# Transposing q and k by crossbar DMA instead of on TensorE, and reading q in row order in the score matmul

## The chip, the cores and the metric

The kernel runs on one core of a Trainium2 chip. The metric is the device time of one execution in microseconds (us), the median of three runs. TensorE (PE) does the matmuls, VectorE (DVE), ScalarE (ACT) and GpSimd (POOL) the elementwise work; SP and GpSimd issue the DMAs.

## The reference, cut to what matters

A sliding-window attention with a linear distance bias, and behind it a two-layer network with ELU, on all tokens:

```python
B, H, S, D = 8, 8, 576, 64                       # q, k, v: float32
scores = q @ k.T / sqrt(D)                       # per batch and head
bias = slope[h] * -abs(i - j)
mask = (0 <= i - j) & (i - j < 128)              # window of 128 keys
attn = softmax(where(mask, scores + bias, -1e9))
x = attn @ v                                     # (B*S, H*D) = (4608, 512)
h = x @ w_in                                     # 512 -> 2048
g = where(h > 0, h, exp(min(h, 0)) - 1)
out = g @ w_out                                  # 2048 -> 512, (4608, 512) float32
```

## The kernel before, in words

**Slots.** The order of the work is written out by hand. The dictionary `tasks` and the function `at(s, f, ...)` (L510) put calls into numbered slots, and the loop at L589 issues slot after slot. A batch takes 16 slots, batch b the slots 16b to 16b+15. In each slot stand, in this order on TensorE: one hidden group (`hidden`, x by w_in into a bank of PSUM, L451), the value matmuls of the slot before (`values`, L394), the score matmuls of this slot (`scores`, L348), transposes if there are any, and one output group of four matmuls (`output`, g by w_out, L492). Each engine takes its instructions in the order in which they are issued.

**Scores.** Keys stand on the partitions of the result and queries on its columns. The 576 rows are cut into blocks of 128 and a last one of 64; a slot has four score matmuls of 128 columns (slots 0 to 13 of a batch), or eight of 64 columns (slots 14 and 15). So there are 56 matmuls of 128 columns in a batch. ScalarE takes the exponential (L372), VectorE cuts off what lies outside the window by a minimum with `band` (`cut`, L380). In batch 0 the bias is added by further matmuls (L368); from batch 1 on it stands in rows 64 to 127 of QK as extra terms of the product.

**The order of rows.** q and k are loaded by GpSimd (`load_qk`, L80) so that partition p gets rows 4p to 4p+3: a run of 1 KB per head, converted to float16. Transposing 128 columns of this (two rows of 64) on TensorE gives columns for rows 4p+j. `transposes` (L307) does it for two heads at a time, eight matmuls (L312) into a PSUM tile of the ring that the scores use too (two buffers, tag "sps"). Two copies per call bring it into QK, by ScalarE for odd pairs of heads (L322) and by VectorE for even ones (L324). In QK the rows of a block of 128 stand in the order j, i: all rows 4i, then all 4i+1, and so on. So the attention's result, x, and the output have their rows in this order too. v is placed in it as well (`place_v4`, L116, batches 0 to 2; `load_v` and `cast_v`, L126 and L134, from batch 3 on). A store of 128 rows of `out` is therefore cut into pieces by `rows_of` (L467): four of 32 rows with a step of four rows in HBM, or fewer where the last block of 64 rows is in it (L498).

**Where the preparation stands.** For batch b+1 the four calls of `transposes` stand in slots 5, 9, 10 and 13 of batch b (9, 10, 13 and 14 of batch 1; 14, 14, 15, 15 of batch 0), and `transposes_tail` for the last 64 rows in slot 14.

**Behind the attention.** `normalize` (L414, L415) divides by the row sums into xn; one slot later `turn` (L418) brings xn into the ring xT, which the hidden groups read: by TensorE in batches 0 and 1, by a crossbar transpose on SP's queue (L423) from batch 2 on. ScalarE takes exp of the hidden group (L455), GpSimd cuts it to 0 to 1 (L456), VectorE makes g (`elu`, L463) one slot later. The hidden groups have two buffers in PSUM.

**Queues.** SP issues the loads of v from batch 3 on, the turns of xn and the stores. GpSimd issues the loads of q and k, the tails and v of the first batches, between its own work: e (L456) and casts of v (L134).

Of the kernel before, what the change touches and what calls it, by code (L numbers as in the profile page):

```python
# [9 lines left out]
F16 = mybir.dt.float16  # L10
I32 = mybir.dt.int32
AF = mybir.ActivationFunctionType
ALU = mybir.AluOpType
# [6 lines left out]
def kernel(  # L20
# [9 lines left out]
    nc = tc.nc  # L30
    B, H, S, D = q.shape
    NTOK, DO = out.shape
    FF = moe_w_in.shape[1]
    NP = H // 2
# [6 lines left out]
    V = nc.vector  # L41

    const = ctx.enter_context(tc.tile_pool(name="const", bufs=1))
    stage = ctx.enter_context(tc.tile_pool(name="stage", bufs=2))
# [8 lines left out]
    def one(shape, dt, name):  # L53
        return const.tile(shape, dt, name=name, tag=name)
# [18 lines left out]

    stq, stt, vf, vs = {}, {}, {}, {}

# [73 lines left out]
    with tc.manual_schedule():  # L149

        row = one([128, 1], I32, "row")
        col = one([128, 128], I32, "col")
        posi = one([128, 576], I32, "posi")
        nc.gpsimd.iota(row, pattern=[[0, 1]], base=0, channel_multiplier=1)
        nc.gpsimd.iota(col, pattern=[[1, 128]], base=0, channel_multiplier=0)
        load_half(0, 1, 0)
# [16 lines left out]
        rowf = small("rowf")  # L173
        V.tensor_copy(rowf, row)
        V.tensor_scalar(out=ident, in0=col, scalar1=rowf, scalar2=None, op0=ALU.is_equal)
        for h in range(H):
# [25 lines left out]

        seen(0, posi[:, 0:256], kpos, 0, 256)
        unseen(0, 128, 0.0, ALU.is_gt)
# [3 lines left out]
        def last_blocks():  # L208
            seen(256, posi[:, 512:576], kpos, -384, 64)
            seen(320, posi[:, 512:576], rowf, -512, 64)  # L210
            unseen(256, 64, -127.0, ALU.is_lt)
            unseen(320, 64, 0.0, ALU.is_gt)
            join(256, 128)
# [93 lines left out]
        def transposes(b, hp):  # L307
# [8 lines left out]
            for odd in range(2):  # L316
# [6 lines left out]
                else:  # L323
                    V.tensor_copy(o, i)  # L324

        def transposes_tail(b):
            t = ps_s.tile([128, NP, 2, 64], F16, name="tpt", tag="sps")
# [12 lines left out]
        def scores(b, s):  # L340
# [6 lines left out]
            def mm(o, h, kc, qc, n):  # L347
                nc.tensor.matmul(t[:, o:o + n], qk[0:r, h, 1, kc:kc + 128], qk[0:r, h, 0, qc:qc + n],  # L348
                                 start=b > 0 or o == 0, stop=b > 0)
# [116 lines left out]

        def rows_of(c0):  # L467

            r = []
            c = c0  # L470
            while c < c0 + 128:
                b, o = divmod(c, S)
                if o < 512:
                    n, p = divmod(o, 128)
                    r.append((c - c0, out[b * S + 128 * n + p // 32:b * S + 128 * n + 128:4, :]))
                    c += 32
                else:
                    r.append((c - c0, out[c:c + 64, :]))
                    c += 64
            return r  # L480

        def output(t, j):
# [11 lines left out]
            if f0 == 12:  # L494
                ob = work.tile([128, DO], F32, name="ob", tag="ob")
                nc.scalar.copy(ob, ops[t])  # L496
                for p0, rows in rows_of(512 * t + 128 * ts):
                    nc.sync.dma_start(rows, ob[p0:p0 + rows.shape[0], :])  # L498

# [10 lines left out]
        def at(s, f, *a):  # L510
            tasks.setdefault(s, []).append((f, a))
# [15 lines left out]
        for b in range(B):  # L527
# [16 lines left out]
            if b + 1 < B:  # L544
                for hp in range(NP):
                    at(s0 + ((5, 9, 10, 13) if b > 1 else (9, 10, 13, 14) if b else (14, 14, 15, 15))[hp],
                       transposes, b + 1, hp)
                at(s0 + (14 if b else 25), transposes_tail, b + 1)
# [34 lines left out]
        at(18, load_v4, 2)  # L583
        at(33, load_v4_tail, 2)
        for n in range(4):
            at(15 + n, place_v4, 1, n)
            at(32 + n, place_v4, 2, n)

# [39 lines left out]
```

The softmax here doesn't subtract the row's maximum and nothing guards it: scores larger than these inputs give would overflow.

## Time and profile before

| | |
|---|---|
| median of the runs | 366.17 us (366.01 to 367.24) |
| the profiled execution | 365.46 us, its span 363.7 us |
| TensorE busy | 340.3 us |
| VectorE busy | 243.5 us |
| ScalarE busy | 206.7 us |
| GpSimd busy | 145.7 us |
| transposes L312, in number | 224 (7 batches of 32) |
| stores, in number | 136 |

A line of a group gives: line, engine, operation, output <- input, shapes, count, then busy us and mean ns of one, then the engine's idle time just before them and what ended it. A line of a timeline gives start, us, engine, line, operation, and in brackets idle time before it and its releaser. Matmuls are pipelined: the mean time of one contains its latency, and the pace of a stream is read from the starts. A digit of the slices is the busy share of a fortieth of the span, in tenths.

### The profile page before, as it was taken

The numbers are of one execution on the slowest core, as the hardware profiler recorded it, in microseconds if no ns is written. First come the engines' busy times: TensorE is split into PE (matmuls) and PEld (weight loads), VectorE is DVE, ScalarE is ACT, GpSimd is POOL, SyncE is SP. The second block draws the span as 40 slices with busy tenths as digits, with TensorE's granted clock in tenths as the row PEclk, the third lists the DMA queues.
The fourth block names the chain that finished last, engine by engine and source line by source line (L and its number), as shares of the span: only waits on it lengthen the run. The fifth ranks groups of instructions, "written<-read, shape, count | busy, mean of one in ns | idle before, by whom it ended". The sixth has DMA issues, their size and how long they took to land.

```text
span 363.7 us, 9613 instructions
## 1 busy us (share of the span) xinstructions
PE 340.3 (94%) x3790; PEld 251.6 (69%) x3790; DVE 243.5 (67%) x574; ACT 206.7 (57%) x349; POOL 145.7 (40%) x229
## 2 busy tenths in 40 slices
PE   6878997999979999989999999999999999999994
PEld 6766775777647667767777777777777777666651
DVE  6479889678886776666676767776776756634430
ACT  4355583666537655765566665666567565543431
POOL 9146623434314723472346334642433232233320
PEclk9899999999999999999999999999999999999999
DMA  8999999839243973497448934793631222211113
GB/s 114 198 206 119 228 107 183 151 80 155 38 103 89 133 108 84 110 128 110 98 94 127 127 88 100 120 136 82 102 84 45 52 47 45 51 43 47 29 43 73
DMA packets 81948, 37.06 MB, mean 102 GB/s; under 512 B 51952, under 2 KB 77296, under 8 KB 81904
## 3 DMA queue, kind: packets, MB, share of 16 engines
q0 software_dynamic: 34064, 15.40, 35.5%
q1 hardware_dynamic: 47840, 21.06, 25.6%
q8 instruction: 29, 0.48, 0.6%
q14 instruction: 15, 0.12, 0.1%
HBM read 36.70 MB, written 9.44 MB: 127 GB/s over the span
## 4 chain that ended last, share of the span: by engine, by line
PE 65%; DVE 14%; ACT 9%; DMA 7%; issue 3%; POOL 1%; SPq 0%; ACTq 0%; POOLq 0%
PE hp L451 27%; PE op L492 25%; PE sp L348 5%; ACT QK L322 5%; DVE VP L116 4%; DMA vs<-in_v_dram 3%; PE av L394 3%; DVE g L463 3%; ACT EX L372 2%; DVE QK L324 2%; ACT e L455 2%; DVE EX L380 2%; DMA xT<-xn 2%; DMA stq<-in_q_dram 1%; DVE xn L415 1%
## 5 line engine op out<-in xcount | busy, mean ns | idle before, releaser
L456 POOL TENSOR_SCALAR e<-e 128x512 f32<-128x512 f32 x144 | 88.6, 615 | 199.9 <-ACT e L455 199.9
L451 PE MATMUL hp<-xT,wi 128*128 128x256 f16 (+3 forms) x1536 | 150.3, 246 | 8.1 <-DVE g L463 3.6
L451 PEld LDWEIGHTS <-wi 128*128 128x128 f16 x1536 | 121.5, 98 | 49.9 <-DVE g L463 5.5
L455 ACT ACTIVATE e<-hp 128x512 f32<-128x512 f32 x144 | 86.0, 597 | 119.0 <-PE hp L451 110.0
L492 PE MATMUL op<-wo,g 128*128 128x512 f16 x576 | 146.4, 379 | 0.0
L463 DVE SCALAR_TENSOR_TENSOR g<-e,hp 128x512 f16<-128x512 f32 x144 | 98.0, 681 | 23.9 <-POOL e L456 22.7
L380 DVE TENSOR_TENSOR EX<-EX,band 128x512 f16<-128x512 f16 x112 | 49.8, 445 | 57.1 <-ACT EX L372 57.0
L372 ACT ACTIVATE EX<-sp 128x512 f16<-128x512 f32 x128 | 75.9, 593 | 13.3 <-PE sp L368 8.6
L492 PEld LDWEIGHTS <-g 128*128 128x128 f16 x576 | 51.2, 98 | 36.9
L348 PE MATMUL sp<-QK 128*128 128x128 f16 (+3 forms) x576 | 49.8, 213 | 0.0
L394 PE MATMUL av<-VP,EX 128*128 128x65 f16 x576 | 38.6, 193 | 4.3 <-DVE EX L380 2.7
L394 PEld LDWEIGHTS <-EX 128*128 128x128 f16 x576 | 31.6, 98 | 8.7 <-DVE EX L380 4.2
L415 DVE TENSOR_TENSOR xn<-av,rden 128x256 f16<-128x256 f32 x80 | 34.0, 424 | 2.8
L348 PEld LDWEIGHTS <-QK 128*128 128x128 f16 (+1 forms) x576 | 31.3, 97 | 1.0 <-issue 0.2
L496 ACT COPY ob<-op 128x512 f32<-128x512 f32 x36 | 21.1, 586 | 14.3 <-PE op L492 6.4
L322 ACT COPY QK<-tp 64x1024 f16<-64x1024 f16 x28 | 28.1, 1005 | 1.6 <-PE tp L312 1.4
L414 DVE RECIPROCAL rden<-av 128x4 f32<-128x4 f32 x80 | 14.4, 180 | 16.0 <-PE av L394 14.6
L134 POOL TENSOR_SCALAR VP<-vf 128x512 f16<-128x512 f32 (+1 forms) x25 | 19.5, 779 | 2.7 <-DMA vf<-in_v_dram 2.7
L324 DVE COPY QK<-tp 64x1024 f16<-64x1024 f16 x28 | 19.2, 684 | 1.1 <-PE tp L312 0.8
L312 PE MATMUL tp<-ident,stq 128*128 128x128 f16 x224 | 17.1, 219 | 2.3 <-ACT QK L322 1.0
L312 PEld LDWEIGHTS <-stq 128*128 128x128 f16 x224 | 13.8, 98 | 3.4 <-issue 3.2
L116 DVE COPY VP<-vs 32x512 f16<-32x512 f16 x48 | 14.9, 310 | 1.3 <-DMA vs<-in_v_dram 0.5
(70 smaller groups left out, 118.5 us busy)
## 6 DMA issues: line engine op xcount, KB each, us to landing
out_dram<-ob SPq DMA_DIRECT2D x128, 64.0 KB, 1.7
vf<-in_v_dram SPq DMA_DIRECT2D x80, 64.0 KB, 2.3
stq<-in_k_dram POOLq DMA_DIRECT2D x7, 512.0 KB, 6.4
stq<-in_q_dram POOLq DMA_DIRECT2D x7, 512.0 KB, 7.5
wi<-in_moe_w_in_dram POOLq DMA_DIRECT2D x4, 512.0 KB, 13.8
wo<-in_moe_w_out_dram POOLq DMA_DIRECT2D x4, 512.0 KB, 15.1
QK<-TQ SPq DMA_DIRECT2D x2, 576.0 KB, 8.0
vs<-in_v_dram POOLq DMA_DIRECT2D x2, 512.0 KB, 9.9
```

The source lines that it names most:

```text
L312: nc.tensor.transpose(t[:, g, w, :, j, :], stq[b][:, w, 2 * hp + g, 2 * j:2 * j + 2, :].rearrange("p a d -> p (a d)"), ident)
L322: nc.scalar.copy(o, i)
L348: nc.tensor.matmul(t[:, o:o + n], qk[0:r, h, 1, kc:kc + 128], qk[0:r, h, 0, qc:qc + n], start=b > 0 or o == 0, stop=b > 0)
L372: nc.scalar.activation(e[:, 0:512], t, AF.Exp, scale=0.125)
L380: V.tensor_tensor(out=e, in0=e, in1=band[:, c:c + n].unsqueeze(1).broadcast_to([128, 512 // n, n]), op=ALU.min)
L394: nc.tensor.matmul(a[:, l, :], e[:, c:c + 128], vp[:, n, h, 0:D + 1], start=st, stop=sp)
L415: V.tensor_tensor(out=xnt[b, i][:, 4 * half:4 * half + 4, :], in0=a[:, :, 0:D], in1=r.unsqueeze(2).broadcast_to([128, 4, D]), op=ALU.mult)
L451: nc.tensor.matmul(p[:, l * w + u0:l * w + u1], w_in_sb[:, c, fc * 128:(fc + 1) * 128], xT[:, c, x0:x0 + u1 - u0], start=(c == 0), stop=(c ...
L455: nc.scalar.activation(e, p, AF.Exp)
L456: nc.gpsimd.tensor_scalar(out=e, in0=e, scalar1=1.0, scalar2=0.0, op0=ALU.min, op1=ALU.max)
L463: V.scalar_tensor_tensor(out=gs[t][:, f0:f0 + nf, c0:c0 + w], in0=sh(es.pop((t, j))), scalar=1.0, in1=sh(hps.pop((t, j))), op0=ALU.subtrac ...
L492: nc.tensor.matmul(ops[t], gs[t][:, fc, ts * 128:(ts + 1) * 128], w_out_sb[:, fc, :], start=(fc == 0), stop=(fc == NFC - 1))
```

## The change

For batches 2 to 7 `transposes` is no longer called. In its place stand two new functions, eight calls of each per batch:

- `cross(b, n)` issues one crossbar transpose on SP's queue: from 128 partitions of stq, two heads of q or of k (512 columns of float16), to the tile tq in SBUF, of which there is one buffer. For batches 3 to 7 they stand in slots 0 to 7 of the batch before, for batch 2 in slots 22 to 25, two in each.
- `uncross(b, n)` copies from tq to QK on VectorE, for one j and all heads: 64 partitions by 1024 elements, float16, SBUF to SBUF. They stand in slots 5 to 12 of the batch before, for batch 2 in slots 28 to 31, two in each.

The layout of QK stays as it was. The score matmuls with 128 columns now read q through a rearranged pattern: four elements with a step of 32, then the next four. So the columns of the scores, and all that follows from them, have q's rows in their own order; the window and the distances of the first blocks are made from `col` instead of `posi`. Each store of 128 rows is one DMA, and `rows_of` is gone. The tail load of v of batch 2 moves from slot 33 to 22, and its placement from slots 32 to 35 to slots 24, 26, 28 and 30.

```diff
-        col = one([128, 128], I32, "col")
+        col = one([128, 256], I32, "col")
...
-        seen(0, posi[:, 0:256], kpos, 0, 256)
+        seen(0, col, kpos, 0, 256)
...
+        def cross(b, n):
+
+            w, hp = 1 - n // NP, n % NP
+            if n == 0:
+                tq[b] = stage.tile([128, 2, H, 2, 128], F16, name="tq", tag="tq", bufs=1)
+            nc.sync.dma_start_transpose(
+                out=tq[b][:, w, 2 * hp:2 * hp + 2, :, :].rearrange("p h a c -> p (h a) c"),
+                in_=stq[b][:, w, 2 * hp:2 * hp + 2, :, :].rearrange("p h j d -> p (h j d)"))
+
+        def uncross(b, n):
+            w, j = 1 - n // 4, n % 4
+            r = slice(64 * (j % 2), 64 * (j % 2) + 64)
+            V.tensor_copy(
+                QK[b % 2][0:64, :, w, 0:512].rearrange("p h (n j i) -> p h n j i", j=4, i=32)[:, :, :, j, :],
+                tq[b][r, w, :, j // 2, :].rearrange("p h (n i) -> p h n i", i=32))
...
-                nc.tensor.matmul(t[:, o:o + n], qk[0:r, h, 1, kc:kc + 128], qk[0:r, h, 0, qc:qc + n],
+                m = qk[0:r, h, 0, qc:qc + n]
+                if n == 128:
+                    m = m.rearrange("p (j i) -> p i j", j=4)
+                nc.tensor.matmul(t[:, o:o + n], qk[0:r, h, 1, kc:kc + 128], m,
                                  start=b > 0 or o == 0, stop=b > 0)
...
-                for p0, rows in rows_of(512 * t + 128 * ts):
-                    nc.sync.dma_start(rows, ob[p0:p0 + rows.shape[0], :])
+                r = 512 * t + 128 * ts
+                nc.sync.dma_start(out[r:r + 128, :], ob)
...
-                for hp in range(NP):
-                    at(s0 + ((5, 9, 10, 13) if b > 1 else (9, 10, 13, 14) if b else (14, 14, 15, 15))[hp],
-                       transposes, b + 1, hp)
+                if b == 0:
+                    for hp in range(NP):
+                        at((14, 14, 15, 15)[hp], transposes, b + 1, hp)
+                else:
+                    for n in range(8):
+                        at(s0 + (n if b > 1 else 6 + n // 2), cross, b + 1, n)
+                        at(s0 + (5 + n if b > 1 else 12 + n // 2), uncross, b + 1, n)
...
-        at(33, load_v4_tail, 2)
+        at(22, load_v4_tail, 2)
         for n in range(4):
             at(15 + n, place_v4, 1, n)
-            at(32 + n, place_v4, 2, n)
+            at(24 + 2 * n, place_v4, 2, n)
```

More of the change, by code (lines that the diff above doesn't have):

```diff
@@ L71 @@
     xT = one([128, 4, RING], F16, "xT")
-    stq, stt, vf, vs = {}, {}, {}, {}
+    stq, stt, vf, vs, tq = {}, {}, {}, {}, {}
     def load_qk(b, w, h0=0, h1=H):
@@ L151 @@
         row = one([128, 1], I32, "row")
-        col = one([128, 128], I32, "col")
+        col = one([128, 256], I32, "col")
         posi = one([128, 576], I32, "posi")
         nc.gpsimd.iota(row, pattern=[[0, 1]], base=0, channel_multiplier=1)
-        nc.gpsimd.iota(col, pattern=[[1, 128]], base=0, channel_multiplier=0)
+        nc.gpsimd.iota(col, pattern=[[1, 256]], base=0, channel_multiplier=0)
         load_half(0, 1, 0)
@@ L174 @@
         V.tensor_copy(rowf, row)
-        V.tensor_scalar(out=ident, in0=col, scalar1=rowf, scalar2=None, op0=ALU.is_equal)
+        V.tensor_scalar(out=ident, in0=col[:, 0:128], scalar1=rowf, scalar2=None, op0=ALU.is_equal)
         for h in range(H):
@@ L208, in last_blocks @@
         def last_blocks():
-            seen(256, posi[:, 512:576], kpos, -384, 64)
-            seen(320, posi[:, 512:576], rowf, -512, 64)
+            seen(256, col[:, 0:64], kpos, 128, 64)
+            seen(320, col[:, 0:64], rowf, 0, 64)
             unseen(256, 64, -127.0, ALU.is_lt)
@@ L465, in elu @@
                 in1=sh(hps.pop((t, j))), op0=ALU.subtract, op1=ALU.max)
[L467 to L480, printed above, removed]
         def output(t, j):
```

## The prediction

> **What bounds the kernel now.** I read the page first: busy shares, slices, chain, groups.
>
> ```profile
> PE 340.3 (94%) x3790; PEld 251.6 (69%) x3790; DVE 243.5 (67%) x574; ACT 206.7 (57%) x349; POOL 145.7 (40%) x229
> PE   6878997999979999989999999999999999999994
> DMA  8999999839243973497448934793631222211113
> PE 65%; DVE 14%; ACT 9%; DMA 7%; issue 3%; POOL 1%; SPq 0%; ACTq 0%; POOLq 0%
> ```
>
> TensorE is full from about slice 8 on. A busy TensorE need not be TensorE at its peak, so I looked in the timeline for the pace of one slot: from one hidden group to the next.
>
> ```profile
> 244.35 1.04 PE L451 MATMUL hp<-xT,wi 128*128 128x256 f16 x8
> 245.22 0.29 PE L394 MATMUL av<-VP,EX 128*128 128x65 f16 x4
> 245.35 0.38 PE L348 MATMUL sp<-QK 128*128 128x128 f16 x4
> 245.57 1.03 PE L492 MATMUL op<-wo,g 128*128 128x512 f16 x4
> 246.44 1.04 PE L451 MATMUL hp<-xT,wi 128*128 128x256 f16 x8
> ```
>
> The starts are 2.09 us apart with no wait in brackets. The four score matmuls hold the engine from 245.35 to 245.57: 0.22 us, 55 ns each. A slot with transposes looks so:
>
> ```profile
> 228.34 0.39 PE L348 MATMUL sp<-QK 128*128 128x128 f16 x4
> 228.93 0.61 PE L312 MATMUL tp<-ident,stq 128*128 128x128 f16 x8 [0.21 <-ACT QK L322]
> 229.38 1.03 PE L492 MATMUL op<-wo,g 128*128 128x512 f16 x4
> ```
>
> Eight transposes hold TensorE for 0.45 us, and before them it waits 0.21 us for a score buffer that ScalarE still empties. The kernel has its own control: while batch 7 is scored, nothing is left to transpose. In the same timeline, hidden groups 16 slots apart start at 242.15 and 278.94 (batch 6 scored, batch 7 prepared: 36.79 us), then at 278.94 and 312.63 (batch 7 scored: 33.69 us). Preparing a batch so costs 3.10 us: 4 x 0.45 = 1.80 of transposes, 0.33 of tail transposes (which stay), the rest, 0.97, waits around the copies.
>
> The groups by line and the DMA issues of the page price what is exchanged (count, busy us, mean ns; for a DMA the us from issue to landing), and the waits of SP's queue (us, times, longest) show its room:
>
> ```profile
> L348 PE MATMUL sp<-QK 128*128 128x128 f16 (+3 forms) x576 | 49.8, 213 | 0.0
> L322 ACT COPY QK<-tp 64x1024 f16<-64x1024 f16 x28 | 28.1, 1005 | 1.6 <-PE tp L312 1.4
> L324 DVE COPY QK<-tp 64x1024 f16<-64x1024 f16 x28 | 19.2, 684 | 1.1 <-PE tp L312 0.8
> L116 DVE COPY VP<-vs 32x512 f16<-32x512 f16 x48 | 14.9, 310 | 1.3 <-DMA vs<-in_v_dram 0.5
> xT<-xn SPq DMA_TRANSPOSE x30, 2.4
> ```
>
> ```profile
> SPq L498 <- ACT ob L496: 149.2, 34, 16.9
> ```
>
> SP has spent 149.2 us waiting for output tiles, so it has time to give. All 30 crossbar transposes of xn have the size of the new ones (128 x 512) or half of it: the trace of before prices them.
>
> [...]
>
> **The change part by part.** Sums are against the profiled execution (365.46 us, span 363.7, so 1.8 around it); the median of the runs, 366.17, lies 0.7 above it.
>
> 1. Transposes of batches 2 to 7 leave TensorE. By the control, each preparation gives back 3.10 − 0.33 = 2.77 us, in which some 0.2 of waits at the tail may stay. Five are made in the packed stretch: 13.8. Batch 2's, while batch 1 is scored, has 4 x 0.45 and 0.6 of waits: 2.4. Together **−16.2**.
>
> 2. 48 crossbar transposes on SP: 1.19 us of its queue each, 2.4 to landing, 9.5 us of queue per batch. What leaves is store issues: four at 0.42 become one, some 1.3 us for each of 4.5 stores, 5.7 per batch. The rest there is 5 turns (6.0), 17 loads of v (about 9.4) and stores (1.9): in all 26.8 of 33.7 us, so the queue keeps up over a batch. It does not within slots 0 to 7: 8 transposes 9.5, three groups of v loads 6.6, two turns 2.4, two stores 0.9 make 19.4 against 16.7, a lag of some 3 us. Queued behind it: turn (L423), whose landing the hidden groups of slot s+3 wait for in batches 2 and 3 (they already wait 1.4 us there), and loads of v, which cast_v on GpSimd takes three slots (6.3 us) later. Loads land in 2.3, so casts keep 1 to 2 us of their three slots; if they lose it, e (L456) stands behind them, and g behind e. Of waits that are added: the transposes wait for the single tq to be free, which is so from slot 12, and for stq, loaded 14 slots before (batch 2's 5 to 6 slots, 10 us, against 7.5 to landing); each copy waits for a transpose issued 5 slots, 10 us, before, against 3 of lag and 2.4 of landing. I charge **+1.0**; bounds 0 and +5 (each of four early turns 1.2 late).
>
> 3. 48 VectorE copies of 64 x 1024 in SBUF. [...] by L324, which reads PSUM, 684. I take 0.45[...]. Eight per batch, 3.6 us, replace four of 684 (2.7) on VectorE and four of 1005 on ScalarE. In slots 5 to 10, a pair of slots has two g (1.36), two min (0.89), one reciprocal and xn (0.60), two copies (0.9): 3.75 of 4.17 us. Covered; with 0.684 each it would be 4.22, the point where the cover is gone, at about 0.05 per pair. The next g and rden stand behind each copy, the hidden matmuls of two slots on behind g[...]. Batch 2's copies come two to a slot in 28 to 31, in slots 28 and 30 with the four VP copies (1.17): VectorE then needs about 12.7 us in four slots of 2.1 to 2.3, an excess near 4. In the kernel before, the VP copies stood in slots 32 to 35 and TensorE waited 3.0 us there (0.32, 0.23, 0.87, 1.62). So that stall moves, and I charge **+0.5** net (bounds −3 and +2). The earlier tail load on POOL's queue writes rows that batch 0 gave up in slot 16: nothing.
>
> 4. Whole stores: hidden until the last under TensorE's stream, since a third buffer of ob comes round only after 3 x 4 slots, 25 us. There three issues (1.2 us in sequence) become one, but 256 KB land later than 64 (1.7) or 128 (2.4): by that step about 3.8 us. **+0.5**; bounds −1 and +1.
>
> 5. The setup reads another iota, 256 columns in place of 128 (0.23 us for those): nothing, beside the first loads; 0.2 if they did not cover it.
>
> 6. The score matmuls with n = 128 read q with a step of 32 elements, 64 bytes, four in turn[...]. There are 56 per batch, 448. No row has such a read. Below: free, 0, since 128 columns are still 128; a gain is excluded, as neither work nor waits are fewer. Above: [...] half the rate, so 55 ns more each. Then batches 1 to 7 cost 392 x 0.055 = 21.6, and batch 0, where loads and VectorE end most waits, half of 3.1. A longer slot (2.3) takes about 1 off VectorE's excess in 3. **+22.1**. [...]
>
> Nothing hides item 6: score matmuls stand in the stream that sets the end. I take the upper value[...]. Sum: 365.46 − 16.2 + 1.0 + 0.5 + 0.5 + 22.1 = 373.4; on the median of the runs **374.0 us**.
>
> **The rivals.**
> - The stepped read is free (faster). Everything else stands: 374.0 − 22.1 = 351.9, about 352 us. [...] Its point of decision: items 1 to 4 give 14.2, item 6 takes 22.1 at 55 ns, so they are even at 55 x 14.2 / 22.1 = 35 ns, a matmul of about 1.6 times the present 55; below that the kernel is faster.
> - The read costs something between, 1.2 to 1.7 times: 11 to 39 ns, 356 to 367 us.
> - More than half rate, or half rate and late turns and casts from SP's lag in every batch: 380 to 400. For it: DMA is busy 0.67 of each packed batch against 0.23 in the last one, and transposes landed in up to 6.4 us. Against: SP's 149.2 us of waiting.
> - The change does not do what it says: the program has no transposes of batches 2 to 7 on TensorE any more, so this is out.
>
> **How the numbers follow.** Half rate 0.48 (369 to 379 us by itself, from the bounds in 2 to 4), free 0.37 (347 to 357), between 0.06, worse 0.09. The time of the likeliest is 374. The range from 349 to 379 leaves out the worse case and the lowest part of the free one, under 2 in 10; it is wide because the two large cases lie 22 us apart on either side of the present time. Faster (by over 0.3%, about what a measurement of this kernel can tell from no change): free, and most of between, 0.41. Same: 0.05, from between and the low end of half rate. Slower: 0.54.
>
> **What would show it.** Score matmuls (four of one slot): 0.44 us from the first to the next line's start if the rate is half, 0.22 if free. Slots without other work 2.3 or 2.08 us. Batches 16 slots apart at 36.8 us or 33.7. No L312 after batch 1's, and no wait for ScalarE's QK copies. The uncross copies 0.42 to 0.5 us; TensorE waiting for DVE in slots 28 to 32, some 3 us; for xT 1 to 3 us in all. I am wrong if the score matmuls keep their 55 ns, or if the copies take 0.7 us and VectorE becomes the bound.

## The result, and the profile after

The changed kernel takes 416.44 us (median of four runs, 414.72 to 421.33) against 366.71 for the kernel before, measured beside it: ratio 1.134, interval 1.129 to 1.139. The ratios here and below leave out slow runs, those more than 1.5% above the fastest of the same kernel, such as the 421.33. The prediction was 374.0 us with a range of 349 to 379; the result lies outside it, on the predicted side.

First the page of the changed kernel (span 415.1 us): the busy shares, two rows of slices and the shares of the chain that ended last.

```profile
PE 400.1 (96%) x3598; PEld 266.7 (64%) x3598; DVE 246.4 (59%) x597; ACT 193.4 (47%) x325; POOL 142.3 (34%) x229
...
PE   7989999998899999999999999999999999999996
...
DMA  9997959989235985599546965494441111120102
...
PE 84%; DMA 6%; DVE 4%; SPq 2%; ACT 1%; issue 1%; POOL 0%; ACTq 0%; DVEq 0%; POOLq 0%
PE hp L470 28%; PE op L496 27%; PE sp L367 22%; PE av L413 4%; DMA xT<-xn 4%; SPq L331 2%; DMA out_dram<-ob 1%; PE sp L387 1%; DMA stq<-in_q_dram 1%; PE spare L509 1%; ACT EX L391 1%; DVE VP L116 1%; DVE QK L338 1%; DVE g L482 1%; PE tpt L346 0%
```

TensorE has 192 instructions fewer (3790 to 3598: the transposes of six batches) and is busy 60 us longer. It is full in nearly every slice and holds 84% of the chain where it held 65%; its idle time fell from 23 to 15 us, so no new wait holds it. The last line names the place: the score matmuls, L367, are 22% of the chain. So the next view is the pace of one slot, TensorE's timeline in the packed stretch (start, us, engine, line, operation).

```profile
225.87 1.04 PE L470 MATMUL hp<-xT,wi 128*128 128x256 f16 x8
226.75 0.28 PE L413 MATMUL av<-VP,EX 128*128 128x65 f16 x4
226.87 1.03 PE L367 MATMUL sp<-QK 128*128 128x128 f16 x4
227.72 1.04 PE L496 MATMUL op<-wo,g 128*128 128x512 f16 x4
228.60 0.60 PE L470 MATMUL hp<-xT,wi 128*128 128x256 f16 x4
```

From 226.87 to 227.72 the four score matmuls hold the engine for 0.85 us, 212 ns each, where they held it for 0.22 us, 55 ns each. The slot is 2.73 us long (225.87 to 228.60) instead of 2.09. That is not half the rate but a quarter. Over the kernel this is 448 x 157 ns = 70 us more of TensorE's time; experiment 1 shows what it costs in the kernel's time. The groups and the DMA issues of the same page show what the rest of the change cost (count, busy us, mean ns; idle us ahead of the group and its releaser; for the DMA KB and us to landing):

```profile
L367 PE MATMUL sp<-QK 128*128 128x128 f16 (+3 forms) x576 | 121.3, 345 | 0.9 <-DVE QK L338 0.5
...
L338 DVE COPY QK<-tq 64x1024 f16<-64x1024 f16 x48 | 20.0, 416 | 0.7
...
out_dram<-ob SPq DMA_DIRECT2D x36, 256.0 KB, 2.3
```

The score matmuls' busy time went from 49.8 to 121.3 us. VectorE's copies take 416 ns each and have only 0.7 us of idle time ahead of them in the whole kernel. Among SP's own waits one line answers to the one of before:

```profile
SPq L502 <- ACT ob L500: 166.0, 29, 20.1
```

SP still waits 166.0 us for output tiles. Batch by batch (from the scores of slot 15 to those of the next batch's slot 15, batches 1 to 7, us):

| kernel | 1 | 2 | 3 | 4 | 5 | 6 | 7 |
|---|---|---|---|---|---|---|---|
| before | 43.7 | 38.5 | 38.0 | 36.8 | 36.8 | 36.8 | 33.7 |
| after | 47.3 | 45.8 | 44.3 | 43.0 | 43.0 | 43.1 | 42.7 |

Batch 7, which prepares nothing, is 9.0 us longer: 56 x 157 ns = 8.8. The middle batches are only 6.2 longer, because they no longer transpose on TensorE.

### The profile page after: what moved, and what is told of

Read it like the earlier page. It is cut to its first block, busy times and chain, and to the rows that moved or that the text cites. A ratio compares the mean times of both kernels' runs of the same rounds, so it can differ in the third digit from the quotient of the medians.

```text
span 415.1 us, 9166 instructions
## 1 busy us (share of the span) xinstructions
PE 400.1 (96%) x3598; PEld 266.7 (64%) x3598; DVE 246.4 (59%) x597; ACT 193.4 (47%) x325; POOL 142.3 (34%) x229
## 4 chain that ended last, share of the span: by engine, by line
PE 84%; DMA 6%; DVE 4%; SPq 2%; ACT 1%; issue 1%; POOL 0%; ACTq 0%; DVEq 0%; POOLq 0%
PE hp L470 28%; PE op L496 27%; PE sp L367 22%; PE av L413 4%; DMA xT<-xn 4%; SPq L331 2%; DMA out_dram<-ob 1%; PE sp L387 1%; DMA stq<-in_q_dram 1%; PE spare L509 1%; ACT EX L391 1%; DVE VP L116 1%; DVE QK L338 1%; DVE g L482 1%; PE tpt L346 0%
## 5 line engine op out<-in xcount | busy, mean ns | idle before, releaser
L470 PEld LDWEIGHTS <-wi 128*128 128x128 f16 x1536 | 123.3, 99 | 44.7 <-issue 5.1
L496 PE MATMUL op<-wo,g 128*128 128x512 f16 x576 | 148.8, 383 | 0.0
L367 PE MATMUL sp<-QK 128*128 128x128 f16 (+3 forms) x576 | 121.3, 345 | 0.9 <-DVE QK L338 0.5
L399 DVE TENSOR_TENSOR EX<-EX,band 128x512 f16<-128x512 f16 x112 | 48.9, 437 | 102.4 <-ACT EX L391 102.0
L496 PEld LDWEIGHTS <-g 128*128 128x128 f16 x576 | 58.0, 103 | 57.6 <-issue 0.5
L367 PEld LDWEIGHTS <-QK 128*128 128x128 f16 (+1 forms) x576 | 44.4, 104 | 24.9 <-issue 0.8
L338 DVE COPY QK<-tq 64x1024 f16<-64x1024 f16 x48 | 20.0, 416 | 0.7
L134 POOL TENSOR_SCALAR VP<-vf 128x512 f16<-128x512 f32 (+1 forms) x25 | 15.4, 615 | 1.2 <-DMA vf<-in_v_dram 1.2
L509 PE MATMUL spare<-ident 128*128 128x128 f16 x94 | 9.3, 278 | 1.6 <-DVE ident L175 1.6
L509 PEld LDWEIGHTS <-ident 128*128 128x128 f16 x94 | 8.4, 130 | 1.7 <-DVE ident L175 1.6
L352 DVE COPY QK<-tpt 64x512 f16<-64x512 f16 x16 | 6.7, 418 | 1.1 <-PE tpt L346 1.0
```

Source lines behind the costliest of these rows:

```text
L338: V.tensor_copy(QK[b % 2][0:64, :, w, 0:512].rearrange("p h (n j i) -> p h n j i", j=4, i=32)[:, :, :, j, :], tq[b][r, w, :, j // 2, :].re ...
L399: V.tensor_tensor(out=e, in0=e, in1=band[:, c:c + n].unsqueeze(1).broadcast_to([128, 512 // n, n]), op=ALU.min)
L470: nc.tensor.matmul(p[:, l * w + u0:l * w + u1], w_in_sb[:, c, fc * 128:(fc + 1) * 128], xT[:, c, x0:x0 + u1 - u0], start=(c == 0), stop=(c ...
L496: nc.tensor.matmul(ops[t], gs[t][:, fc, ts * 128:(ts + 1) * 128], w_out_sb[:, fc, :], start=(fc == 0), stop=(fc == NFC - 1))
L509: nc.tensor.matmul(spare[:, 0:128], ident, ident, start=True, stop=True)
```

## The experiments

Theory at the start: the stepped read is the whole loss, and everything else in the change gains. Rival: the crossbar path costs something by itself. Times are medians; each ratio is to the kernel before, run on the same chip.

**1. The crossbar part alone, and the row part alone.** The first kernel is the changed one with the contiguous read, and with it the old order of rows and stores in pieces; the second is the kernel before with the stepped read and whole stores.

```diff
-                m = qk[0:r, h, 0, qc:qc + n]
-                if n == 128:
-                    m = m.rearrange("p (j i) -> p i j", j=4)
-                nc.tensor.matmul(t[:, o:o + n], qk[0:r, h, 1, kc:kc + 128], m,
+                nc.tensor.matmul(t[:, o:o + n], qk[0:r, h, 1, kc:kc + 128], qk[0:r, h, 0, qc:qc + n],
```

> The changed kernel with one part undone: the score matmuls read q contiguously again, so rows stay in the order j, i and a store is cut into pieces of 32 rows; the crossbar transposes, the VectorE copies and the moved placement of v stay. Theory (the stepped read is the whole loss): score matmuls back at 0.22 us for four instead of 0.85, slots of 2.08 us, time 351 to 356 us; the upper end because SP then issues 4 or 3 pieces per store and is full for 32.5 of 33.7 us per batch. Rival (the crossbar path itself costs: SP's queue, DMA traffic, VectorE's copies): the time stays above the kernel before, 368 to 395 us, with new waits of TensorE for xT, QK or g of 10 us or more.

> The kernel before with one part of the change added: the stepped read of q in the score matmuls and whole stores; transposes stay on TensorE. Theory (the stepped read is the whole loss): 448 matmuls x 157 ns = 70 us, less some 5 in batch 0 and 4 to 6 of waits that the longer slots take up: 424 to 432 us. Rival (the stepped read is slow only beside the DMA and VectorE traffic of the crossbar path): under 400 us.

Measured: 407.86 us for the crossbar part alone (ratio 1.107, interval 1.100 to 1.114), 435.47 for the row part alone (one run). The second lies 68.5 us above the kernel before, but not all of that is the read. This kernel and the changed one issue the same work up to slot 15 of batch 0, and yet that slot's scores start at 65.4 us in the row part alone and at 54.6 us in the changed kernel. Here is that stretch in both, first the row part alone (window, length, busy us of PE, PEld, DVE, ACT and POOL with instructions, granted clock, DMA share, GB/s):

```profile
13.00:61.00 48.00, 48.00 (x384) 36.00 (x382) 24.96 (x67) 15.74 (x25) 13.92 (x20) 0.50 0.98 142
13.00:50.00 37.00, 34.56 (x383) 23.66 (x383) 24.96 (x69) 15.66 (x25) 13.81 (x20) 0.95 1.07 162
```

For the same matmuls the row part alone took 48 us at a granted clock of 0.50, the changed kernel 37 us at 0.95. Why the clock stayed low in this run isn't known; from 13 to 61 us it was 0.96 in the changed kernel and 1.00 in the kernel before. Without these 10.8 us the row part costs 57.7 us, and the kernel would stand at 424.7, inside the expectation. From there on the row part alone took 48.9, 45.1, 45.3, 45.0, 45.0, 45.0 and 42.7 us for batches 1 to 7.

The crossbar part alone breaks the theory: with the read back at 0.22 us per slot the kernel should have fallen to about 352 and is 41 us **slower** than before, above even the rival's range. The waits of the crossbar-only kernel (us, times, longest) say where:

```profile
PE hp L467 <- DVE g L479: 44.7, 17, 8.6
DVE QK L338 <- DMA tq<-stq: 42.0, 11, 9.2
```

and its chain, in order of time (start, us, what), shows one such wait whole:

```profile
169.39 0.82 SPq L439
170.26 6.54 DMA tq<-stq
...
177.26 0.68 DVE g L479
177.98 1.86 PE hp L467 x16
```

SP issues the turn of xn, and behind it the crossbar transpose that a copy on VectorE needs. It lands 6.54 us later, the copy has waited 9.2 us by then, g stands behind the copy on VectorE, and the hidden matmuls behind g. In the changed kernel this wait is absent. SP issues fewer pieces of stores there, and each slot is 2.73 us long: two slots between the last transpose and the copy that needs it are 5.5 us, here 4.2. Experiment 3 has a kernel with the same stores as the changed one, and it waits too. So there are two costs, and the slow read hides the other.

**2. Which steps of the moving operand cost.** The changed kernel with another pattern of the moving q in each batch (steps of 1, 2, 4, 8, 16 elements, then runs of 2, 4, 8):

```diff
-                    m = m.rearrange("p (j i) -> p i j", j=4)
+                    m = PATTERN[b](m)
```

> The changed kernel with another moving pattern per batch in the 56 score matmuls of 128 columns; each still reads 128 columns of the same block, in another order, and the window is left open (band passes everything), so the output is not the reference's. Batch 0: contiguous; batches 1 to 4: steps of 2, 4, 8 and 16 elements (4, 8, 16, 32 bytes); batches 5, 6, 7: runs of 2, 4 and 8 contiguous elements, each run 64, 64 and 32 bytes on from the last. Read off: start of the scores to start of the output group, 0.22 us at full rate, 0.43 at half, 0.85 at a quarter. [...] step 2 half, steps 4, 8, 16 a quarter; runs of 2 half, of 4 and 8 full. Any step other than 1 switches to a slow mode: steps 2 to 16 all a quarter, and runs of 2 to 8 a quarter too or full.

Measured in TensorE's timeline, from the first of four score matmuls (L378) to the next line's start (L507); the batches are those with steps of 2, 4 and 8 elements, then runs of 2 and of 4 elements at steps of 64 bytes:

```profile
58.38 0.39 PE L378 MATMUL sp<-QK 128*128 128x128 f16 x4
58.61 1.02 PE L507 MATMUL op<-wo,g 128*128 128x512 f16 x4
...
106.76 0.62 PE L378 MATMUL sp<-QK 128*128 128x128 f16 x4
107.20 0.61 PE L507 MATMUL op<-wo,g 128*128 128x512 f16 x2
...
160.90 1.07 PE L378 MATMUL sp<-QK 128*128 128x128 f16 x4
161.79 0.61 PE L507 MATMUL op<-wo,g 128*128 128x512 f16 x2
...
237.03 0.60 PE L378 MATMUL sp<-QK 128*128 128x128 f16 x4
237.45 0.83 PE L507 MATMUL op<-wo,g 128*128 128x512 f16 x3
...
291.54 0.39 PE L378 MATMUL sp<-QK 128*128 128x128 f16 x4
291.76 0.81 PE L507 MATMUL op<-wo,g 128*128 128x512 f16 x3
```

Subtract the starts of each pair; the table gives the median of the 14 slots of each batch. Batch 0 (contiguous) can't be compared, since the bias matmuls follow its scores; the contiguous row is from the kernel before.

| pattern (float16) | elements used of 16 bytes at a time | four matmuls, us |
|---|---|---|
| contiguous | 8 | 0.22 |
| step 2 | 4 | 0.23 |
| step 4 | 2 | 0.44 |
| step 8, step 16 | 1 | 0.89, 0.91 |
| runs of 2, 64 bytes apart | 2 | 0.42 |
| runs of 4, 64 bytes apart | 4 | 0.22 |
| runs of 8, 32 bytes apart | 8 | 0.22 |

Neither case of the expectation gives this table: step 2 ran at full rate and step 4 at half. The step does not decide, nor do the bytes jumped: what fits all rows is how many elements in a row come from the same 16 bytes. Of 8, 16 and 32 bytes only 16 fits: with 8, step 2 and runs of 2 would both count two elements (0.23 and 0.42 us), with 32, step 4 and runs of 4 would both count four (0.44 and 0.22). In these runs four or eight took 0.22 to 0.23 us, the full rate, two took 0.42 to 0.44, half, and one took 0.89 to 0.91, a quarter. The change takes one.

**3. The row order put elsewhere, or left out.** In the first kernel the read is contiguous and ScalarE's exponential writes the columns in their own order, with a step of four elements; in the second the read is contiguous and the order of the output's rows is simply left out, so that stores stay whole.

```diff
+            if i < 4:
+                o = o.rearrange("p (b i j) -> p b j i", i=32, j=4)
+                x = x.rearrange("p (b j i) -> p b j i", i=32, j=4)
             nc.scalar.activation(o, x, AF.Exp, scale=0.125)
```

> The changed kernel with the order of rows restored in another place: score matmuls read q contiguously, and ScalarE's exponential writes its result in row order (two-byte elements at a step of 4, in place of a contiguous write, from PSUM read in the order of the scores); stores stay whole. If ScalarE writes at a step at its usual pace (0.59 us for L391): 349 to 354 us, under the variant with stores in pieces. If its stepped write costs as the stepped moving read does (four times): ScalarE has 0.6 + 2.4 us in a slot of 2.1 and the time is above 400 us. If twice: 1.2 + 0.6 + 0.15 in a slot of 2.1, close to the bound, 355 to 365 us.

> The changed kernel with the contiguous read of q and whole stores: it differs from the variant with the crossbar part alone (408 us) in the stores only, one DMA in place of three or four; the rows of the output so stay in the order of the scores inside their blocks, which is left out. In that variant TensorE waited 45 us for g, g behind VectorE's copies of q (n = 4 to 7), and these 42 us for the last transposes of q, issued some 6 us behind their slot and landing in 6.5 us. Theory (SP's queue is too full in slots 0 to 9 once slots are 2.1 us long): two stores fewer by 3 DMAs each in those slots take 2.5 us off the lag, so 3 to 4 us less per batch in 5 batches: 380 to 392 us. Rival (it is the pieces of the stores[...]): all is gone, 350 to 356 us. Rival (the transposes themselves are slow beside the loads, wherever they stand): 400 to 408 us.

Measured: 399.94 (ratio 1.090, 1.087 to 1.093) and 395.37 (1.077, 1.071 to 1.084). In the first, the group of the exponential reads

```profile
L398 ACT ACTIVATE EX<-sp 128x512 f16<-128x512 f32 x128 | 157.5, 1230 | 30.9 <-PE sp L370 17.7
```

1230 ns where it was about 595. That mean takes in 16 instructions of the last blocks, which write without a step in 597 ns; the 112 stepped ones take 1321 ns. The stepped write more than doubles ScalarE's time, and with batches of 39.2 us, 2.45 per slot, TensorE is no longer the bound. The expectation's 355 to 365 for a write at half pace did not hold; but the crossbar path is in this time too, and the second kernel, without the stepped write, is only 4.6 us faster. In that second kernel one store in place of four lifts 12.5 us off the crossbar-only kernel (407.86 to 395.37, just above the theory's 380 to 392), so SP's load matters; but 28.8 us of waits for tq stay. It issues the same DMAs as the changed kernel and differs from it in the read: free reading gave 395 us, not 352.

**4. The schedule of transposes and copies.** From the crossbar-only kernel: first the four copies of q moved from slots 9 to 12 to slots 12 to 15; then also the transposes two slots earlier, with a tile each for q and k; then also the stores issued from ScalarE's queue.

```diff
-  at(s0 + (5 + n if b > 1 else 12 + n // 2), uncross, b + 1, n)
+  at(s0 + (5 + n + 3 * (n // 4) if b > 1 else 12 + n // 2), uncross, b + 1, n)
...
-  at(s0 + (n if b > 1 else 6 + n // 2), cross, b + 1, n)
+  at(s0 + (n - 2 if b > 2 else n // 2 if b > 1 else 6 + n // 2), cross, b + 1, n)
...
-  nc.sync.dma_start(rows, ob[p0:p0 + rows.shape[0], :])
+  nc.scalar.dma_start(rows, ob[p0:p0 + rows.shape[0], :])
```

> The variant with the crossbar part alone (408 us; contiguous read, stores in pieces), with one thing changed: for batches 3 to 7 the four VectorE copies of q stand in slots 12 to 15 in place of 9 to 12. A copy of q for one j takes all eight heads, so the first needs all four transposes of q, the last of which is issued in slot 7. Theory (the copies of q stand only two slots behind the last transpose that they need, and VectorE's g behind them): 6.3 us of distance more takes away most of the 42 us of waits: 362 to 374 us. Rival (SP's lag grows from batch to batch, so any distance is used up): 390 us or more. Rival (the crossbar path's cost is elsewhere, in DMA traffic that delays loads and turns): 395 us or more with waits of TensorE for xT or of GpSimd for vf.

> As the variant with the late copies of q, and the transposes too are moved: for batches 4 to 7 two slots earlier (slots 14 and 15 of the batch before, then 0 to 5), for batch 3 two to a slot from slot 0; tq is two tiles, one for k and one for q, so that k's can start while q's copies of the batch before still run. SP has the same work. Theory (bursts in slots 0 to 9 make the lag): transposes done by slot 5 and copies of q from slot 12 leave 14 us between; no wait for tq is left and the time is 352 to 360 us. Rival (SP is full over the whole batch, 32.5 of 33.7 us, and lags anyway): 365 us or more, TensorE waiting for xT.

> As the variant with early transposes and late copies, and the stores (in pieces) are issued by ScalarE's queue in place of SP's: 7.6 us per batch leave SP, and ScalarE, busy 45%, takes them. If SP's lag still costs time there, this is faster by that: 350 to 356 us. If it doesn't, ScalarE's exponentials behind the issues cost 0 to 4 us: 354 to 362 us.

Measured: 401.27 (1.097, 1.089 to 1.106), 400.37 (1.090, 1.083 to 1.096) and 416.05 (1.135, 1.128 to 1.142). In all three the theory misses. The waits of the early-late kernel show why more distance did not help:

```profile
POOL VP L134 <- DMA vf<-in_v_dram: 49.0, 13, 6.6
...
DVE QK L338 <- DMA tq<-stq: 4.4, 2, 2.9
```

The wait for tq fell from 42.0 to 4.4 us, and the wait of GpSimd's casts for the loads of v rose from 8.5 to 49.0. Both are issued by SP; when the one was given more distance, the other became late. With the stores on ScalarE's queue the wait is ScalarE's own, in its list of waits and in its timeline:

```profile
ACT e L471 <- DMA out_dram<-ob: 35.5, 15, 3.5
...
177.46 2.00 ACTq L514 DMA_DIRECT2D out_dram<-ob  x4
179.57 0.60 ACT L471 ACTIVATE e<-hp 128x512 f32<-128x512 f32 x1 [2.14 <-issue]
```

ScalarE computes nothing while its queue issues four pieces for 2.00 us; the exponential of the hidden group stands behind them.

**5. One of SP's customers taken away.** From the early-late kernel, for batches 4 to 7: without SP's loads of v (the casts read old tiles), without the crossbar transposes (VectorE's copies read old tiles), without GpSimd's loads of q and k; and last, the early-late schedule together with whole stores, the order of the rows left out.

> The variant with early transposes and late copies (400 us; contiguous read, stores in pieces) without the loads of v for batches 4 to 7, which is left out (the casts on GpSimd stay and read batch 3's tiles again). In that variant GpSimd waited 49 us for vf, and g, and TensorE behind it. Theory A (SP's queue issues too much: 140 of 180 us, in bursts, and whatever stands last in a burst comes late): 9 us per batch leave SP and the time falls to 355 to 365 us. Theory B (landing is what is slow: transfers take 6.5 us in place of 2.5 while GpSimd's loads of q and k run): waits move from vf to tq and xT, 380 us or more.

> The same variant without the crossbar transposes of batches 4 to 7 (left out; VectorE's copies stay and put batch 3's q and k in place again). Theory A (SP's issue time): 355 to 362 us, and what is left shows what VectorE's copies cost by themselves: next to nothing. Theory B (slow landing beside the loads of q and k): v loads and turns land late still, but their own number is that of the kernel before, so 355 to 365 us too. Rival (VectorE's copies, not the transposes, hold TensorE up): 375 us or more.

> The same variant without GpSimd's loads of q and k (first 512 rows) for batches 4 to 7 (left out; the transposes take batch 2's and 3's tiles again). SP issues all that it did. Theory A (SP's issue time): the bursts lag as before, 385 to 398 us. Theory B (slow landing beside the loads of q and k): no transfer of SP's takes over 4 us in the second half, the waits for vf and tq go, 355 to 365 us. Both together: between, 366 to 384 us.

> Early transposes and late copies with whole stores and a contiguous read (the rows of the output stay in the order of the scores inside their blocks, which is left out). SP issues 5.7 us less per batch than the variant with stores in pieces (400 us). Theory A: 365 to 385 us. Theory B: within 5 us of 400, since the landing stays slow. If SP's lag was only just too much: 352 to 360 us.

Measured, in one run each: 368.72, 368.56, 382.63 and 373.39 us, against 400.37. Taking either customer off SP is worth 32 us, and the same for both; the two lie some 4 and 7 us above theory A's ranges, for the preparation of batches 2 and 3 was left as it was and still costs. In batches 4 to 6 the kernel without transposes, with all the copies, takes 34.0, 34.3 and 34.3 us, hardly more than a batch that prepares nothing (33.7), so the copies on VectorE are not the cost.

SP's issues, added up from its timeline over each of batches 4 to 6, take about 22 us in the kernel before and 32.5 to 33.0 in the crossbar-only and the early-late kernel, which leaves next to no room in 34. With either customer taken away they take 21 to 25. So the queue is too full. But that is not the whole: without GpSimd's loads of q and k SP issues as much as before (31.8 to 33.3 us per batch), and still 18 us are gone, the "both together" of the expectation. Batches 4 to 6 take 37.6 to 38.1 us, and the slowest load of v lands in 4.1 us where it took 6.7. In this schedule a full queue and slow landing beside the loads make the loss together. (The run takes GpSimd's time for issuing these loads away as well, so it doesn't tell their bytes from that.)

With whole stores SP issues 26.5 to 29.4 us per batch. Two of the batches 4 to 6 fall to the pace of a batch that prepares nothing (34.2 and 34.0 us): there the crossbar path is hidden altogether. The one between takes 41.7, with a load of v that lands in 5.86 us.

**6. How much crossbar the queue can carry.** What was still open: is SP over-full in every batch, or do only batches 2 and 3 start a lag? These kernels start from the kernel before (reads contiguous, TensorE transposing for batches 1 to 3): crossbar for batches 4 to 7; for 4 and 6 alone; for 4 to 7 with q put into its own order by VectorE and whole stores; and for 4 to 7 with k alone by crossbar, q by two calls of eight transposes on TensorE.

```diff
+                if b > 2:
+                    for n in range(8):
+                        at(s0 + n - 2, cross, b + 1, n)
+                        at(s0 + 5 + n + 3 * (n // 4), uncross, b + 1, n)
+                else:
...
+                    for hq in range(2):
+                        at(s0 + (10, 13)[hq], transposes_q, b + 1, hq)
```

> The kernel before, with batches 4 to 7 alone prepared by crossbar transposes (slots -2 to 5 of the batch before) and VectorE's copies (k in slots 5 to 8, q in 12 to 15); batches 1 to 3 as before, reads contiguous, stores in pieces. Theory (SP's queue is over-full in bursts whichever batch is prepared): the batches in which batches 4 to 7 are prepared take 41 to 44 us each as in the early-late kernel, against 36.8 to 38 before, so 385 to 390. Rival (the loss lies in the preparation of batches 2 and 3 and runs on from there): each replaced preparation gives back 2.8 us, 366.7 - 4 x 2.8 = 355 to 357.

> As the last, but only batches 4 and 6 are prepared by crossbar, 5 and 7 on TensorE, so that SP's queue has a batch to drain in. Theory: if a burst drains within the next batch, the two cost some 4 to 7 us each (374 to 381); if the lag needed two batches in a row to build up, they gain 2.8 each (361). Rival (early preparation only): 361.

> Batches 4 to 7 prepared by crossbar, and VectorE's copy of q writes it in its rows' own order (a step of 4 elements in SBUF), so that the score matmul reads contiguously and stores are whole from batch 4 on; the extra rows of q and the window are put in that order once. Theory (SP's load decides): SP has some 5 us less per batch; with the batches of the kernel with whole stores and early-late transposes (41, 34, 42, 34 us against 38, 36.8, 36.8, 36.8) about 369, and 355 if the lag goes altogether. If the stepped write doubles VectorE's copy of q (0.42 to 0.8 us) it costs nothing by itself, since these copies stand in four slots with room: rival (VectorE becomes the bound there): TensorE waits for g behind the copies, 2 us a batch more.

> Batches 4 to 7: k by crossbar and VectorE, q by transposes on TensorE (two calls of eight), stores in pieces. SP has 4.8 us of transposes per batch in place of 9.5. Theory (SP's load decides): 17 to 18 us of 36 less 4.8, the bursts fit, half of the gain of each preparation is had, 361 to 364. Rival (any crossbar transpose beside GpSimd's loads delays others): 370 to 378.

Measured:

| crossbar for | us | ratio, interval | batches 3 to 6, us |
|---|---|---|---|
| none (before) | 367.43 | | 38.0, 36.8, 36.8, 36.8 |
| q and k of 4 to 7 | 386.94 | 1.055, 1.047 to 1.063 | 41.6, 44.0, 45.1, 37.6 |
| q and k of 4 and 6 | 376.28 | 1.023, 1.017 to 1.029 | 42.7, 36.8, 40.1, 37.3 |
| q and k of 4 to 7, q in its own order | 391.27 | 1.067, 1.060 to 1.075 | 45.1, 46.5, 42.4, 36.1 |
| **k of 4 to 7** | **361.62** | **0.984, 0.978 to 0.989** | 36.5, 35.3, 38.0, 35.3 |

The rows for 4 to 7 and for 4 and 6 settle that: late batches lose as well, 3.3 to 8.3 us each. The exception is batch 6. It has the same transposes and loads of v on SP, but no later batch is left for GpSimd to load, and it takes 37.6 us against 36.8. That is the pace of the kernel without GpSimd's loads: with this schedule the loads take part in the loss. They need not: in the crossbar-only kernel batch 6 took 44.8 us, though no transpose in it took over 3.0 us to land. SP's timeline in the kernel for 4 to 7 shows the queue (start, us, engine, line; the last field counts the DMAs):

```profile
185.49 1.92 SPq L513 DMA_DIRECT2D out_dram<-ob  x4
187.52 1.19 SPq L438 DMA_TRANSPOSE xT<-xn  x1
188.76 1.26 SPq L331 DMA_TRANSPOSE tq<-stq  x1
190.12 2.01 SPq L126 DMA_DIRECT2D vf<-in_v_dram  x4
192.17 2.50 SPq L331 DMA_TRANSPOSE tq<-stq  x2
194.77 2.01 SPq L126 DMA_DIRECT2D vf<-in_v_dram  x4
196.88 1.92 SPq L513 DMA_DIRECT2D out_dram<-ob  x3
```

Each line starts about 0.1 us after the one ahead of it ends. From 177.63 to 204.1 SP issues without a pause. At 207.69 GpSimd casts v after 5.17 us of waiting for a load. The chain shows that load:

```profile
201.78 5.74 DMA vf<-in_v_dram
```

It was issued late, and landed in 5.74 us, against 2.4 at the median; GpSimd had issued a load of k at 200.92. Half the transposes fit: that wait of the whole kernel, first in the kernel with all, then in the one with k alone,

```profile
POOL VP L134 <- DMA vf<-in_v_dram: 38.1, 9, 6.6
```

```profile
POOL VP L134 <- DMA vf<-in_v_dram: 8.7, 5, 4.7
```

falls from 38.1 to 8.7 us, and this version beats both kernels, by 1.6% the one before (its four runs: 360.57 to 366.14). The version with q in its own order failed on another price, as VectorE's timeline shows (a copy of k, then one of q):

```profile
198.39 0.42 DVE L355 COPY QK<-tq 64x1024 f16<-64x1024 f16 x1
210.37 1.31 DVE L355 COPY QK<-tq 64x1024 f16<-64x1024 f16 x1
```

A write with a step of four elements takes 1.31 us where the write in runs takes 0.42 (all 16 of them take 1.29 to 1.63). The expectation allowed 0.8. Its wait for loads of v also stays at 33.2 us, so whole stores do not empty SP enough where the transposes come.

**7. What is left in the version with k alone.** One of the two copies behind each call on q goes to ScalarE and one to VectorE, where before both of a call went to one engine; then the same with batch 3 too.

```diff
-                (nc.scalar.copy if hq else V.tensor_copy)(o, i)
+                (nc.scalar.copy if odd else V.tensor_copy)(o, i)
```

> The kernel with k alone by crossbar, but of the two copies behind each call of eight transposes of q one goes to ScalarE and one to VectorE, where before both of a call went to one engine. In the kernel before this one TensorE waited 2.79 us once for g in the slot behind two ScalarE copies of 1.0 us. Theory (that wait is the rest of the cost in the 38.0 us batch): 358 to 360. Rival (the wait is SP's again, a v load, and only shows there): 361 to 363.

> As the last, with batch 3 prepared so too. Theory (half the transposes fit on SP in any batch): a further 1 to 1.5 us, 357 to 359. Rival (early batches have no room on SP or GpSimd): a loss of 2 to 6 us in batch 2, 362 to 366.

Measured: 368.09 (1.003, 1.000 to 1.005) and 366.02 (0.997, 0.995 to 1.000). The first is a clear miss, 6 us slower than with undivided copies (measured on another chip; the ratios, 1.003 and 0.984, say the same). Its batches 3 to 6 take 38.4, 36.6, 37.6 and 36.6 us. Its waits have a line that the other lacks:

```profile
ACT QK L354 <- DVE QK L354: 9.9, 8, 2.1
```

ScalarE's copy waits for VectorE's, in the order in which they were issued, up to 2.1 us; meanwhile ScalarE stands, and the score buffer stays taken. That this makes the 6 us is likely, but not shown. With batch 3 prepared so too the time falls by 2.1 us, somewhat more than the 1 to 1.5 expected, but 366.02 is far from the 357 to 359; with undivided copies this was not tried.

## Why the prediction was wrong, point by point

**Transposes off TensorE (item 1).** Right in kind, and too large under the slow read. From slot 15 of batch 0 on, the row part alone and the whole change differ by items 1 to 3: 317.0 − 309.2 = 7.8 us over batches 1 to 7, where the prediction had −16.2 + 1.0 + 0.5 = −14.7. In batches 4 to 6 the gain is 2.0 us each, not 2.77. That is 4 x 0.45 of transposes and little else: in the row part alone a batch with preparation is only 2.3 us longer than batch 7 (45.0 against 42.7), 0.33 of it tails, so most of the 0.97 of waits around the copies was already gone. The prediction added up a gain and a cost that take up the same waits.

**The stepped read (item 6): the step that failed.** The place was right, L367, and that nothing hides it. The size was not: "half the rate, so 55 ns more each" was 157 ns more each: 70 us of TensorE's time by the pace of the starts, and 57.7 us of the kernel's time by the row part alone (without its slow stretch), against 22.1. The half rate was the author's estimate; no trace of before showed a stepped read. Experiment 2 shows half rate for two elements from the same 16 bytes (0.44 and 0.42 us), a quarter for one (0.89), and the full rate for four (0.23 and 0.22); a step of 4 already halved it. The case of less than half the rate had 0.09 in the prediction. With 57.7 in place of 22.1 and 0.5 the sum is 374.0 + 35.1 = 409; with 7.8 in place of 14.7 for items 1 to 3 as well it is 416.0, which must come near the result, since both are measured. Of the 42 us that the prediction missed, the read with its whole stores is 35.

**The crossbar on SP's queue (item 2): wrong, and hidden.** The text had "each copy waits for a transpose issued 5 slots before". A copy takes one j of all eight heads, so the copy of slot 9 needs the transposes of slots 4 to 7; the last was issued two slots before, not five. At 2.09 us per slot that is 4.2 us against 3 of lag and 2.4 of landing, by the prediction's own numbers too little. The crossbar-only kernel paid for it: 42.0 us of waits. In the changed kernel the waits are absent, and only the read tells it from the kernel with whole stores (395 us, 28.8 us of waits). The likely reason is that it spreads the same issues over 43 us per batch instead of 34; no run tests that alone. So the rival "free read, 352 us" would have been wrong as well: without the slow read the same transposes and copies gave 408 us, and 395 with whole stores. The sum of 26.8 us of issues was right as a mean (26.2 to 28.2 in batches 4 to 6 of the changed kernel), and "the queue keeps up over a batch" did not follow from it. Two readings beside it were off. The loads of q and k stand 6 and 8 slots ahead of the first transposes, not 14, which did no harm in the changed kernel. And "DMA is busy 0.67 of each packed batch" holds for batches 3 to 5 (0.64 to 0.68), not for batch 6 (0.40).

**VectorE's copies (item 3).** Right: 416 ns measured, 450 charged. The 450 was the author's estimate; the trace of before showed VectorE's copies of this size only out of PSUM, at 684 ns. They cost next to nothing where transposes were left out (34.0 to 34.3 us per batch against 33.7, with tails in it). TensorE's waits in slots 28 to 32 were three, 0.49, 1.67 and 0.55 us, 2.7 in all against the 3 named.

**Whole stores (item 4).** A whole store lands 2.3 us after its issue (median of 36; the last ones 2.0 to 2.4), not 3.8. Small. Their larger worth is SP's time, 12.5 us between the two kernels that differ in it, where SP is short of time.

**What stays open.** Preparing batches 2 and 3 by crossbar cost 10 us even where SP had room later on (47.8 and 44.7 us for batches 1 and 2 in the kernel without loads of v, against 43.7 and 38.5). Which of SP, GpSimd's loads and VectorE's placing of v, all crowded there, decides this was not settled. Nor was the share of the full queue and of the slow landing in later batches, or why loads land slowly there.

## What to carry to other kernels

Before reading a matmul's operand in another order, count how many neighbouring elements it takes from each 16 bytes: here four of float16 cost no more than eight (0.22 us for four matmuls), and one cost four times that (0.89). A queue that is four fifths full as a mean may keep up (two batches of the early-late kernel with whole stores) or fall behind in bursts (28.8 us of waits with the first schedule). Ask of each transfer when it is issued and what else is landing then, and check every customer of that queue, for more distance for one can make another late (waits of 42.0 us for tq fell to 4.4, and those for v rose from 8.5 to 49.0). Two bottlenecks can hide each other: test each part of a change alone before saying that a part is free. And look at the clock before subtracting two runs.

## What the runs showed of the hardware that was not expected

After TensorE had waited 8.6 us, it came back slower. Three stretches of the crossbar-only kernel (window, length, busy us of each engine with instructions, granted clock, DMA share, GB/s):

```profile
177.90:180.00 2.10, 2.02 (x22) 1.92 (x22) 1.99 (x6) 0.12 (x1) 0.00 (x0) 0.50 0.63 154
180.00:181.00 1.00, 1.00 (x8) 0.59 (x6) 0.00 (x0) 0.89 (x2) 0.42 (x1) 0.55 0.43 87
181.00:183.00 2.00, 2.00 (x29) 1.62 (x28) 1.78 (x4) 0.64 (x2) 1.66 (x3) 1.00 0.03 8
```

The granted clock is 0.50 until about 3 us after the wait and then 1.00 again; the 16 hidden matmuls of the first slot stand in the chain with 1.86 us, those of the next with 0.89. So this wait cost more than its length. Half clock does not need a wait, though: the row part alone had it from 13 to 61 us, while TensorE was busy all the time. And a step of four float16 elements on the writing side has a price on both other engines: ScalarE's exponential 1321 ns in place of 597, VectorE's copy 1.31 us in place of 0.42.
